# A new written-out order for the first stage of an attention and two-MLP kernel

## The chip, the cores and the metric

The kernel runs on one core of a Trainium2 chip. The time is the device time of one execution in microseconds (us). The engines are named as in the profile: PE multiplies matrices (PEld is its weight load, which runs beside it), DVE and ACT work on tiles elementwise, POOL is hardly used here, and SP issues the transfers (DMA). Each engine works through its own list of instructions in order and waits, where it must, for semaphores of the others.

## The reference

For 8 batches, 8 heads, 576 positions and 64 values a head, attention is computed inside chunks of 64 positions only. Its result, as 4608 rows of 512, goes through a gated MLP without an activation, and then through a second MLP with a leaky activation that has a slope per channel:

```
scores = q_c @ k_c.T / 8                 # per chunk of 64, F32
attn   = exp(scores - max); attn = attn / (sum + 1e-9)
x      = (attn @ v_c), heads side by side          # [4608, 512]
y      = (((x @ w1) * (x @ w2)) @ w3) @ w_out      # d_ff 1024
h      = y @ w_in                                  # d_ff 2048
out    = (max(h, 0) + alpha * min(h, 0)) @ w_out2
```

The weights arrive as 64-bit floats.

## The kernel before

Rows are handled in 9 blocks of 512. A **unit** is half a block of attention (256 rows); units 0 and 1 make block 0, units 2 and 3 block 1, and so on. Every product of two matrices is done in three passes over operands that are split in a high and a low half, so one 128-row group of a projection is 4 x 3 = 12 matmuls of 128x512. The operand pair of a block's attention is the tile `x`, of which there are two; block 2's `x` is block 0's buffer and can be written only when block 0's projections are done.

The work up to the first `acc` matmul, the **first stage**, follows a table of steps, `STARTUP`, that is written out by hand. Each step is a letter and an index:

- attention of unit u: `S` scores (PE), `M` maximum (DVE), `X` 16 exps (ACT), `Y` the division (DVE), `T` transpose (PE), `P` copy of the transposed (ACT), `V` product with v (PE), `c` high half of `x` (ACT), `d` low half of `x` (DVE). `q` issues a unit's loads. The order S M X Y T P V c d is a chain.
- weight granule i, a conversion from 64-bit floats: `A` (ACT, also issues the load of granule i+2), `B` (DVE, three instructions), `C` (ACT), `D` (DVE, two), `E` (DVE, two). There are 40: 0 to 15 are w1 and w2, 16 to 23 w_out, 24 to 39 w3. The raw bits of at most three granules are in memory at a time, so granule i+3 can be loaded when `D` of granule i is done.
- block b, group f: `a` and `b` (PE, 12 matmuls each, products with w1 and w2), `k` (ACT copies `a` out), `m` (DVE multiplies, SP writes the result to DRAM). `a` of group f needs granule 2f, `b` granule 2f+1. Blocks 0 to 2 are done here, 48 such groups of 12.
- `h` f.half (PE, 12 matmuls each, 16 in all) folds w3 and w_out into one matrix `wc`, with granule 24+2f+half; `s` and `w` (ACT, DVE) copy it out.

After the table, block 0's results are loaded again (`load_g`), and the `acc` matmuls begin. From there PE is kept in the order of the program; before that point the compiler's scheduler may move instructions on every engine, so that the table is a proposal. The queue of SP is one, in order, too. The first loads come unit by unit:

```
    for u in range(4):
        load_unit(u)
        if u < RAW:
            convert_load(u)
```

The v of a unit is loaded in six pieces, since for odd head pairs the two halves of the rows change places; exps and the product with v (`h2 ^ (a & 1)`, `h2 ^ odd`) follow that.

Of the kernel before, what the change touches and what calls it, by code (L numbers as in the profile page):

```python
# [34 lines left out]

STARTUP = """
    S0 M0 X0 A0 S1 Y0 M1 T0 P0 B0 X1 V0 D0 c0 Y1 C0 A1 d0 T1 A2 E0 P1 S2 B1 V1 A3 c1 M2 C1 d1 X2 D1 S3 B2 a0.0 M3 C2
    Y2 X3 E1 T2 D2 b0.0 B3 P2 Y3 k0.0 V2 C3 A4 m0.0 T3 c2 E2 P3 d2 a0.1 A5 D3 B4 V3 k0.1 E3 C4 c3 D4 b0.1 A6 d3 q4
    q5 E4 a1.0 m0.1 A7 B5 a0.2 k1.0 B6 C5 D5 C6 b1.0 D6 k0.2 E5 E6 A8 b0.2 m1.0 A9 B7 a1.1 m0.2 C7 D7 B8 a0.3 k1.1
    E7 C8 D8 A10 b1.1 k0.3 B9 E8 C9 b0.3 m1.1 A11 D9 B10 a1.2 m0.3 C10 E9 a0.4 k1.2 D10 A12 B11 b1.2 k0.4 E10 C11  # L40
    D11 A13 b0.4 m1.2 E11 B12 A14 a1.3 m0.4 C12 D12 a0.5 B13 k1.3 E12 C13 b1.3 D13 k0.5 A15 B14 E13 b0.5 C14 m1.3
    A16 D14 a1.4 m0.5 E14 B15 A17 a0.6 k1.4 B16 C15 D15 b1.4 C16 k0.6 D16 E15 b0.6 m1.4 A18 E16 B17 a1.5 A19 m0.6
    C17 D17 a0.7 k1.5 B18 E17 C18 b1.5 k0.7 D18 A20 B19 b0.7 m1.5 C19 E18 D19 A21 a1.6 m0.7 E19 S4 B20 k1.6 A22 b1.6
    M4 C20 D20 X4 B21 a1.7 m1.6 E20 b1.7 D21 k1.7 C21 Y4 A23 m1.7 T4 E21 P4 B22 A24 V4 B23 C22 c4 D22 C23 d4 E22 S5
    D23 A25 M5 E23 X5 B24 B25 D24 C24 C25 Y5 A26 E24 T5 P5 D25 h0.0 A27 B26 E25 C26 V5 D26 A28 h0.1 c5 B27 d5 C27 s0
    E26 a2.0 w0 A29 D27 h1.0 k2.0 B28 E27 C28 b2.0 D28 A30 B29 h1.1 m2.0 C29 E28 D29 A31 a2.1 s1 B30 w1 C30 E29 h2.0
    k2.1 D30 A32 B31 b2.1 E30 C31 D31 A33 h2.1 m2.1 E31 a2.2 s2 B32 A34 w2 C32 D32 h3.0 k2.2 B33 E32 C33 b2.2 D33
    A35 B34 h3.1 m2.2 C34 E33 D34 a2.3 A36 s3 B35 w3 C35 h4.0 E34 k2.3 D35 A37 b2.3 B36 E35 C36 h4.1 m2.3 A38 D36
    B37 a2.4 s4 E36 C37 w4 A39 h5.0 D37 k2.4 B38 E37 b2.4 C38 D38 B39 h5.1 m2.4 C39 E38 a2.5 s5 D39 w5 E39 h6.0 k2.5
    b2.5 h6.1 m2.5 a2.6 s6 w6 h7.0 k2.6 b2.6 h7.1 m2.6 a2.7 s7 w7 b2.7 k2.7 m2.7  # L50
# [8 lines left out]
def tile_attention_moe_moe(ctx: ExitStack, tc: tile.TileContext, qkv: bass.AP, w12: bass.AP,  # L59
# [150 lines left out]

    x_t = {}
    un = {}

    def load_unit(u):
# [4 lines left out]
        else:  # L219
# [3 lines left out]
                 "e": granule(slots[3], "e", F32).rearrange("p j (a h k) -> p j a h k", a=4, h=2)}  # L223
        v = un[u]["v"]
        for j in range(2):
            nc.sync.dma_start(out=un[u]["qk"][j], in_=qkv[2 * u + j, :, 0:2])
        for j in range(2):
            vs = qkv[2 * u + j, :, 2].rearrange("p (a x) -> p a x", a=4)
            nc.sync.dma_start(out=v[:, j, 0::2], in_=vs[:, 0::2])
            nc.sync.dma_start(out=v[0:D, j, 1::2], in_=vs[D:P, 1::2])  # L230
            nc.sync.dma_start(out=v[D:P, j, 1::2], in_=vs[0:D, 1::2])

    def attn_scores(u, where="att"):
        s = un[u]["s"] = pair(where, "sc")
        for j in range(2):
            q, k = (un[u]["qk"][j][:, i].rearrange("p (a c s) -> p a c s", a=4, c=2) for i in range(2))
            for a in range(4):
                for h2 in range(2):
                    for c in range(2):
                        r0, c0, to = D * h2, D * c, (4 * j + a) * D  # L240
                        matmul(s[c0:c0 + D, h2, to:to + D], q[r0:r0 + D, a, c], k[r0:r0 + D, a, c],
                                         start=True, stop=True)

    def attn_max(u):
        mx = un[u]["mx"] = work.tile([P, 2, 8], F32, tag="mx", name="mx")
        nc.vector.tensor_reduce(out=mx, in_=un[u]["s"].rearrange("p h (a k) -> p h a k", k=D), axis=AX.X, op=ALU.max)
        nc.vector.tensor_scalar_mul(mx, mx, -SCALE)  # L247

    def attn_exp(u, tiles=range(2)):
# [4 lines left out]
        for j in tiles:  # L254
            for a in range(4):
                for h2 in range(2):
                    n, h = 4 * j + a, h2 ^ (a & 1)
                    nc.scalar.activation(out=e[:, j, a, h], in_=s[:, h2, n * D:(n + 1) * D], func=AF.Exp,  # L258
                                         bias=mx[:, h2, n:n + 1], scale=SCALE, accum_out=sm[:, j, a, h:h + 1])

    def attn_softmax(u):
        e, sm = un[u]["e"].rearrange("p j a h k -> p (j a h) k"), un[u].pop("sm").rearrange("p j a h -> p (j a h)")
        nc.vector.tensor_scalar_add(sm, sm, 1e-9)
        nc.vector.reciprocal(sm, sm)
        nc.vector.tensor_tensor(out=e, in0=e, in1=sm.unsqueeze(2).to_broadcast([P, 16, D]), op=ALU.mult)

    def attn_transpose(u, where="att"):
        e = un[u]["e"]
        pa = un[u]["pa"] = pair(where, "pa")
        for j in range(2):  # L270
            for a in range(4):
                transpose(pa[:, j, a * P:(a + 1) * P], e[:, j, a].rearrange("p h k -> p (h k)"), ident)

    def attn_copy(u):
        pt = un[u]["pt"] = work.tile([P, 2, 4, 2, D], F32, tag="pt", name="pt", bufs=1)
        nc.scalar.copy(pt.rearrange("p j a c s -> p j (a c s)"), un[u]["pa"])

# [12 lines left out]
    def attn_out(u, lo):  # L290
# [25 lines left out]
    def fold_split(f, lo):  # L316
        if not lo:
            wc_g[f] = granule(24 + f, "wc")
        dst, ps = wc_g[f], ab["fold"][:, f % 2]
        if lo:  # L320
            nc.vector.tensor_tensor(out=dst[:, LO], in0=ps, in1=dst[:, HI].bitcast(F32), op=ALU.subtract)
        else:
            nc.scalar.copy(dst[:, HI], ps)
# [6 lines left out]
    def product(b, f, a, ps):  # L330
        nc.vector.tensor_tensor(out=a, in0=ps, in1=a, op=ALU.mult)  # L331
# [38 lines left out]
    def proj2(b, f):  # L370
# [6 lines left out]
        nc.vector.tensor_scalar(out=g, in0=ps, scalar1=0.0, scalar2=alpha_sb[:, f:f + 1], op0=ALU.min, op1=ALU.mult)  # L377
        nc.vector.scalar_tensor_tensor(out=g, in0=ps, scalar=0.0, in1=g, op0=ALU.max, op1=ALU.add)  # L378
# [99 lines left out]
    for b in range(LEAD, NB):  # L478
        parts = [p for i in range(2) for p in unit_steps(2 * (b + 1) + i, False)] if b + 1 < NB else []
        for f in range(NF1):  # L480
# [5 lines left out]
            nc.scalar.copy(a, pa)  # L486
# [80 lines left out]
```

## Time and profile before

| what | us |
|---|---|
| median of 3 runs (1537.49 to 1541.13) | 1538.48 |
| the profiled execution | 1539.19 |
| span in it, first to last instruction | 1537.4 |
| PE busy in it | 1494.1 |
| DVE busy | 780.4 |
| ACT busy | 422.6 |

The times come from unprofiled executions, the rows below from one profiled execution, whose own time is 1.8 us over its span. PE is busy for 97% of the span; the rest, and the stretches in which PE ran at the lower of its two clocks, lie almost all in the first 320 us.

### The profile page before, as it was taken

What the parts mean: (1) busy time and instruction counts of PE and PEld (TensorE: products, weight loads), DVE (VectorE), ACT (ScalarE), POOL (GpSimd) and SP (SyncE); (2) the same over time, 40 slices, a digit from 0 to 9 for tenths busy, and PEclk for the clock granted to TensorE, in tenths of its full rate; (3) what the DMA queues carried; (4) which work ended last, traced back from release to release, by engine and by line L of the source; (5) the groups of instructions that cost most, each with busy time, mean ns of one, the idle gap of its engine ahead of it and who ended that gap; (6) DMA issues with size and microseconds to landing.
All of it is one profiled execution on the core that took longest, in us unless ns stands there. A gap on an engine that the chain in (4) does not pass through costs nothing.

```text
span 1537.4 us, 21112 instructions
## 1 busy us (share of the span) xinstructions
PE 1494.1 (97%) x8688; PEld 1231.1 (80%) x8688; DVE 780.4 (51%) x1250; ACT 422.6 (27%) x1107; POOL 0.7 (0%) x6
## 2 busy tenths in 40 slices
PE   4997999999999999999999999999999999999998
PEld 3785787788888888888888888888888888888887
DVE  4989963366667665331334344343434344343433
ACT  6535323444444443331211111111111111111111
POOL 0000000000000000000000000000000000000000
PEclk9998999999999999999999999999999999999999
DMA  8644425644545456236501000010101000000000
GB/s 249 190 165 151 136 98 165 192 153 155 188 163 192 151 179 206 83 103 199 165 0 55 1 20 36 1 55 0 56 0 38 18 7 35 1 28 0 28 1 28
DMA packets 65041, 141.89 MB, mean 92 GB/s; under 512 B 6833, under 2 KB 25265, under 8 KB 64945
## 3 DMA queue, kind: packets, MB, share of 16 engines
q1 hardware_dynamic: 64944, 140.54, 27.7%
q8 instruction: 68, 1.11, 0.3%
q14 instruction: 29, 0.23, 0.0%
HBM read 98.57 MB, written 41.94 MB: 91 GB/s over the span
## 4 chain that ended last, share of the span: by engine, by line
PE 89%; DVE 4%; DMA 3%; ACT 2%; SPq 1%; issue 1%; ACTq 0%; DVEq 0%
PE acc L93 38%; PE a L93 23%; PE b L93 22%; PE wc L93 2%; PE ab L93 2%; DMA v<-in_qkv 1%; ACT e L258 1%; PE sc L93 1%; PE pa L93 1%; DMA raw<-in_wo 1%; DMA raw<-in_w 1%; PE pa L98 1%; DVE p L175 1%; DMA g<-g_dram 1%; DVE m L164 0%
## 5 line engine op out<-in xcount | busy, mean ns | idle before, releaser
L93 PE MATMUL acc<-w,gs 128*128 128x512 f32 x1728 | 414.7, 389 | 0.0
L93 PEld LDWEIGHTS acc<-w,gs 128*128 128x128 f32 x1728 | 324.4, 188 | 67.2
L104 ACT CAST gs<-g 128x512 fp32r<-128x512 f32 x168 | 104.6, 622 | 660.7 <-DVE g L378 635.0
L93 PE MATMUL acc<-gs,wc 128*128 128x512 f32 x864 | 210.2, 395 | 3.8 <-DVE gs L105 3.8
L93 PE MATMUL a<-y,w 128*128 128x512 f32 x864 | 207.5, 389 | 0.0
L93 PE MATMUL b<-y,w 128*128 128x512 f32 x864 | 207.5, 389 | 0.0
L93 PEld LDWEIGHTS acc<-gs,wc 128*128 128x128 f32 x864 | 161.6, 189 | 40.4 <-DVE gs L105 5.5
L93 PEld LDWEIGHTS b<-y,w 128*128 128x128 f32 x864 | 162.2, 188 | 33.7
L93 PEld LDWEIGHTS a<-y,w 128*128 128x128 f32 x864 | 162.2, 188 | 33.7
L105 DVE TENSOR_TENSOR gs<-g,gs 128x512 fp32r<-128x512 f32 x168 | 116.2, 692 | 134.7 <-ACT gs L104 132.7
L93 PE MATMUL a<-x,wa 128*128 128x512 f32 x720 | 175.1, 393 | 2.4 <-DVE x L297 2.4
L93 PE MATMUL b<-x,wa 128*128 128x512 f32 x720 | 175.7, 393 | 0.0
L93 PEld LDWEIGHTS a<-x,wa 128*128 128x128 f32 x720 | 136.3, 190 | 31.3 <-DVE x L297 2.9
L93 PEld LDWEIGHTS b<-x,wa 128*128 128x128 f32 x720 | 133.5, 188 | 27.6
L377 DVE TENSOR_SCALAR g<-b,alpha_sb 128x512 f32<-128x512 f32 x72 | 54.0, 750 | 177.7 <-PE b L93 177.7
L377 DVE TENSOR_SCALAR g<-a,alpha_sb 128x512 f32<-128x512 f32 x72 | 54.0, 750 | 162.6 <-PE a L93 162.6
L258 ACT ACTIVATE e<-sc,mx 128x64 f32<-128x64 f32 x288 | 85.7, 348 | 31.4 <-DVE mx L247 31.4
L331 DVE TENSOR_TENSOR a<-b,a 128x512 f32<-128x512 f32 x60 | 41.3, 688 | 95.1 <-PE b L93 84.4
L258 ACT ACTIVATION_READ_ACCUMULATOR e<-sc,mx 128x1 f32 x288 | 69.7, 242 | 0.0
L93 PE MATMUL ab<-x,wa 128*128 128x512 f32 x288 | 69.3, 390 | 0.0
L486 ACT COPY a<-a 128x512 f32<-128x512 f32 x48 | 28.6, 596 | 131.2 <-PE a L93 112.5
L93 PEld LDWEIGHTS ab<-x,wa 128*128 128x128 f32 x288 | 53.9, 188 | 11.2
(56 smaller groups left out, 995.9 us busy)
## 6 DMA issues: line engine op xcount, KB each, us to landing
qk<-in_qkv SPq DMA_DIRECT2D x36, 512.0 KB, 4.9
raw<-in_w2nd SPq DMA_DIRECT2D x32, 512.0 KB, 4.0
w_dram<-wm SPq DMA_DIRECT2D x32, 512.0 KB, 3.3
w<-w_dram SPq DMA_DIRECT2D x32, 512.0 KB, 3.3
y_dram<-y SPq DMA_DIRECT2D x36, 256.0 KB, 2.9
yraw<-y_dram SPq DMA_DIRECT2D x18, 512.0 KB, 4.3
out<-o SPq DMA_DIRECT2D x36, 256.0 KB, 2.1
raw<-in_w SPq DMA_DIRECT2D x16, 512.0 KB, 4.2
```

Source lines behind the costliest of these rows:

```text
L93: ins = nc.tensor.matmul(*args, **kw)
L98: ins = nc.tensor.transpose(*args, **kw)
L104: nc.scalar.copy(dst[:, HI], src)
L105: nc.vector.tensor_tensor(out=dst[:, LO], in0=src, in1=dst[:, HI].bitcast(F32), op=ALU.subtract)
L175: nc.vector.scalar_tensor_tensor(out=p, in0=conv_raw[i][:, :, 0], scalar=2.0 ** -52, in1=p, op0=ALU.mult, op1=ALU.mult)
L258: nc.scalar.activation(out=e[:, j, a, h], in_=s[:, h2, n * D:(n + 1) * D], func=AF.Exp, bias=mx[:, h2, n:n + 1], scale=SCALE, accum_out=sm ...
L331: nc.vector.tensor_tensor(out=a, in0=ps, in1=a, op=ALU.mult)
L377: nc.vector.tensor_scalar(out=g, in0=ps, scalar1=0.0, scalar2=alpha_sb[:, f:f + 1], op0=ALU.min, op1=ALU.mult)
L486: nc.scalar.copy(a, pa)
```

## The change

The table is written in a new order, and now DVE and ACT are kept to the program's order inside the first stage as PE is (the class `InOrder`, switched off for DVE and ACT after the table). Units 4 and 5 (steps S4 to V5) stand among block 0's and block 1's products, and their `c` and `d` behind block 0's last product. For units 0 to 3 (`u < CROSS`) v is loaded plainly, one transfer per tile, and the heads keep their places. The first loads are regrouped: queries and keys of two units and the first raw weights ahead of v. A first activation of one element (`warm`) brings the table of exps in at once. The folds `h` alternate between two pairs of banks (`att`, `p23`) and stand mostly at the end; the first two reloads of block 0's results (`g0`, `g1`) come before the last `s` and `w`.

```
 STARTUP = """
-    S0 M0 X0 A0 S1 Y0 M1 T0 P0 B0 X1 V0 D0 c0 Y1 C0 A1 d0 T1 A2 E0 P1 S2 B1 V1 A3 c1 M2 C1 d1 X2 D1 S3 B2 a0.0 M3 C2
...
+    S0 A0 M0 B0 X0 S1 D0 M1 A1 Y0 X1 B1 T0 D1 C1 Y1 P0 C0 V0 E1 A2 E0 T1 c0 B2 P1 d0 C2 V1 D2 E2 S2 c1 A3 d1 A4 M2
+    a0.0 B4 X2 b0.0 D4 B3 D3 a0.1 C4 Y2 C3 A5 k0.0 S3 E4 k0.1 E3 T2 M3 b0.1 P2 m0.0 B5 X3 D5 V2 m0.1 a0.2 c2 Y3 A6
...
+    class InOrder:
...
+            def call(*args, **kw):
+                ins = op(*args, **kw)
+                if self.on:
+                    tc.keep_in_program_order(ins)
...
+    CROSS = 4
...
+            if u < CROSS:
+                nc.sync.dma_start(out=v[:, j].rearrange("p a x -> p (a x)"), in_=qkv[2 * u + j, :, 2])
+                continue
...
-                    n, h = 4 * j + a, h2 ^ (a & 1)
+                    n, h = 4 * j + a, h2 ^ (a & 1 if u >= CROSS else 0)
...
-            if f % 2 == 0:
-                ab["fold"] = pair("p23", "wc")
-        ps = ab["fold"][:, f % 2]
+            ab["fold", f] = pair(("att", "p23")[f % 2], "wc")[:, 0]
+        ps = ab["fold", f]
...
+    act.activation(out=work.tile([P, 1], F32, tag="warm", name="warm", bufs=1), in_=ident[:, 0:1], func=AF.Exp)
     for u in range(4):
-        load_unit(u)
-        if u < RAW:
-            convert_load(u)
+        unit_tiles(u)
+    for load, n in ((load_qk, 0), (convert_load, 0), (load_qk, 1), (load_v, 0), (convert_load, 1), (load_v, 1),
+                    (load_qk, 2), (convert_load, 2), (load_v, 2), (load_qk, 3), (load_v, 3)):
+        load(n)
...
-    lent = {0: "att", 1: "p23", 2: "att", 3: "p23"}
+    lent = {1: "p23", 3: "p23", 5: "p23"}
...
-    pinned[0] = True
+    act.on = dve.on = False
     load_unit(2 * LEAD)
-    steps = [(b, f) for b in range(LEAD) for f in range(NF1)]
-    load_g(*steps[0])
-    load_g(*steps[1])
```

What stands in the lists of the engines follows at three places. First SP's queue at the start of the program (`qk` are queries and keys, `raw` raw weights); before:

```order
L226 DMA qk<-in_qkv 128x1024 x2
L229 DMA v<-in_qkv 128x2x128
L230 DMA v<-in_qkv 64x2x128
L231 DMA v<-in_qkv 64x2x128
L229 DMA v<-in_qkv 128x2x128
L230 DMA v<-in_qkv 64x2x128
L231 DMA v<-in_qkv 64x2x128
L143 DMA raw<-in_w 128x1024
L226 DMA qk<-in_qkv 128x1024 x2
```

And of the change:

```order
L238 DMA qk<-in_qkv 128x1024 x2
L148 DMA raw<-in_w 128x1024
L238 DMA qk<-in_qkv 128x1024 x2
L244 DMA v<-in_qkv 128x512 x2
L148 DMA raw<-in_w 128x1024
L244 DMA v<-in_qkv 128x512 x2
L238 DMA qk<-in_qkv 128x1024 x2
```

Unit 1's queries and keys moved from ninth behind six pieces of v to the fourth transfer, and a unit's v is two transfers instead of six.

Next PE around units 4 and 5 (`sc` are scores, `pa` first the transpose, then the product with v, `a`, `b` and `ab` the products of blocks 0 to 2, `wc` the folds), before:

```order
L93 MATMUL b<-x,wa 128x512 x12
L93 MATMUL ab<-x,wa 128x512 x24
L98 MATMUL pa<-ident,e 128x128 x8
L93 MATMUL pa<-pt,v 64x64 x32
L93 MATMUL sc<-qk 64x64 x32
L93 MATMUL wc<-wo,w_1485 128x512 x12
L98 MATMUL pa<-ident,e 128x128 x8
L93 MATMUL wc<-wo,w_1571 128x512 x4
L93 MATMUL pa<-pt,v 64x64 x32
L93 MATMUL wc<-wo,w_1571 128x512 x8
L93 MATMUL a<-x,wa 128x512 x12
```

And of the change, where the scores of both units stand further ahead:

```order
L100 MATMUL a<-x,wa 128x512 x12
L100 MATMUL b<-x,wa 128x512 x12
L100 MATMUL pa<-ident,e 128x128 x16
L100 MATMUL ab<-x,wa 128x512 x12
L100 MATMUL pa<-pt,v 64x64 x32
L100 MATMUL ab<-x,wa 128x512 x12
L100 MATMUL pa<-pt,v 64x64 x32
L100 MATMUL a<-x,wa 128x512 x12
L100 MATMUL b<-x,wa 128x512 x12
L100 MATMUL ab<-x,wa 128x512 x24
```

The transposes and products with v of both units now have products of blocks 0 and 1 in front, between and behind; before, all products of blocks 0 and 1 were done by then.

Last PE at the end of the first stage (`acc` are the first matmuls after the table), of the change:

```order
L100 MATMUL b<-x,wa 128x512 x12
L100 MATMUL ab<-x,wa 128x512 x24
L100 MATMUL wc<-wo,w_2072 128x512 x12
L100 MATMUL wc<-wo,w_2095 128x512 x12
L100 MATMUL wc<-wo,w_2141 128x512 x12
L100 MATMUL wc<-wo,w_2205 128x512 x12
L100 MATMUL wc<-wo,w_2225 128x512 x12
L100 MATMUL acc<-gs,wc 128x512 x12
L100 MATMUL sc<-qk 64x64 x32
```

Before, a fold and a product took turns up to the end, and a product of block 2 stood directly ahead of `acc`; now five folds do.

## Rows read from the trace of the kernel before

**Rows 1.** Busy time of each engine by stretch, with PE's granted clock and DMA.
```profile
core 0: us, PE busy (x) PEld busy (x) DVE busy (x) ACT busy (x) POOL busy (x), PEclk, DMA share, GB/s
0.00:37.57 37.57, 15.71 (x400) 13.84 (x400) 17.93 (x32) 22.35 (x101) 0.70 (x6) 0.96 0.83 253
37.57:56.34 18.77, 17.59 (x199) 13.96 (x195) 16.48 (x31) 13.80 (x52) 0.00 (x0) 0.90 0.76 233
56.34:124.58 68.24, 68.24 (x300) 56.23 (x300) 62.73 (x122) 25.81 (x43) 0.00 (x0) 1.00 0.49 164
124.58:163.86 39.28, 27.33 (x343) 21.34 (x343) 37.53 (x72) 24.47 (x87) 0.00 (x0) 0.83 0.36 117
163.86:242.90 79.04, 79.04 (x349) 65.15 (x347) 50.65 (x94) 20.88 (x35) 0.00 (x0) 1.00 0.43 138
242.90:245.30 2.40, 0.01 (x2) 0.00 (x1) 1.44 (x3) 1.82 (x3) 0.00 (x0) 1.00 0.39 144
245.30:319.12 73.82, 72.65 (x548) 58.09 (x549) 26.66 (x39) 29.33 (x94) 0.00 (x0) 0.98 0.49 153
319.12:1537.40 1218.28, 1213.55 (x6557) 1002.50 (x6555) 567.02 (x862) 284.14 (x694) 0.00 (x0) 1.00 0.22 74
```

**Rows 2.** The chain that ended last: start us, length us, engine and tile.
```profile
59.37 2.72 PE ab L93 x12
81.50 4.98 DMA raw<-in_w
146.94 4.84 ACT e L258 x32
249.90 1.09 PE sc L93 x64
267.54 0.87 PE pa L98 x8
```

**Rows 3.** Timeline of PE, to 40 us: start, length, work [idle before <-releaser].
```profile
4.42 1.13 PE L93 MATMUL sc<-qk 64*64 64x64 f32 x32 [4.42 <-DMA qk<-in_qkv]
5.78 1.13 PE L93 MATMUL sc<-qk 64*64 64x64 f32 x32 [0.23 <-DMA qk<-in_qkv]
12.62 1.14 PE L93 MATMUL sc<-qk 64*64 64x64 f32 x32 [5.71 <-DMA qk<-in_qkv]
...
35.65 1.99 PE L93 MATMUL sc<-qk 64*64 64x64 f32 x64 [4.18 <-DVE x L297]
37.57 4.74 PE L93 MATMUL a<-x,wa 128*128 128x512 f32 x12
```

**Rows 4.** What DMA moved in 0 to 37 us, in 40 equal slices.
```profile
GB/s 0 31 217 350 412 344 227 142 248 261 332 399 395 338 231 247 266 215 412 412 351 235 246 267 279 332 394 379 328 193 95 226 213 310 390 407 133 0 0 18
```

**Rows 5.** Timeline of DVE and ACT, first instructions.
```profile
6.98 1.23 DVE L246 TENSOR_REDUCE mx<-sc 128x16 f32<-128x1024 f32 x1 [6.98 <-PE sc L93]
...
8.50 1.28 ACT L258 ACT_TABLE_LOAD   x1 [8.50 <-DVE mx L247]
```

**Rows 6.** Timeline of PE, 140 to 250 us.
```profile
142.54 1.98 PE L93 MATMUL sc<-qk 64*64 64x64 f32 x64 [3.21 <-DVE x L297]
...
149.97 4.39 PE L93 MATMUL wc<-wo,w 128*128 128x512 f32 x10 [3.02 <-DVE w L180]
...
245.30 4.60 PE L93 MATMUL acc<-gs,wc 128*128 128x512 f32 x12 [2.39 <-DVE gs L105]
```

**Rows 7.** Groups by line, 0 to 245 us: busy us, mean ns | idle before <-releasers.
```profile
L164 DVE SCALAR_TENSOR_TENSOR m<-raw,m 128x512 uint32<-128x512 uint32 x40 | 27.5, 687 | 0.6
L155 ACT ACTIVATE m<-raw 128x512 f32<-128x512 f32 x40 | 27.2, 697 | 33.0 <-DMA raw<-in_w3t 13.1 <-DMA raw<-in_wo 9.9 <-DMA raw<-in_w 9.7
L161 DVE TENSOR_SCALAR m<-m 128x512 f32<-128x512 f32 x40 | 16.6, 419 | 5.6 <-ACT m L155 5.6
...
L246 DVE TENSOR_REDUCE mx<-sc 128x16 f32<-128x1024 f32 x6 | 7.3, 1217 | 7.0 <-PE sc L93 7.0
...
L300 ACT CAST x<-pa 128x1024 fp32r<-128x1024 f32 x6 | 6.2, 1027 | 1.1 <-PE pa L93 0.9
```

More of the change, by code (lines that the diff above doesn't have):

```diff
@@ L42 @@
[L42 to L46, printed above, removed]
@@ new lines @@
+    k1.5 E16 b1.5 A18 B17 B18 C17 V4 D18 a1.6 C18 A19 m1.5 E18 b1.6 B19 k1.6 D17 C19 a0.6 E17 m1.6 D19 b0.6 k0.6 E19
+    A20 a0.7 m0.6 B20 A21 B21 C20 b0.7 k0.7 A22 D21 C21 E21 a1.7 c4 m0.7 c5 d4 b1.7 d5 k1.7 D20 E20 a2.0 m1.7 B22
+    b2.0 k2.0 D22 C22 E22 A23 a2.1 B23 A24 m2.0 C23 B24 b2.1 k2.1 D24 C24 A25 D23 a2.2 B25 E23 C25 b2.2 k2.2 m2.1
+    D25 E25 a2.3 m2.2 E24 A26 b2.3 B26 k2.3 D26 C26 h0.0 E26 m2.3 A27 B27 h0.1 A28 D27 C27 E27 A29 h1.0 s0 B29 w0
+    h1.1 D29 C29 E29 A30 B28 a2.4 s1 w1 C28 D28 b2.4 k2.4 E28 B30 h2.0 m2.4 C30 D30 E30 h2.1 A31 B31 A32 D31 C31
@@ L51 @@
+    h3.0 s2 B32 A33 D32 C32 a2.5 B33 D33 C33 b2.5 k2.5 E31 E32 h3.1 w2 m2.5 E33 h4.0 s3 A34 w3 B34 A35 h4.1 D34 C34
+    E34 A36 a2.6 B36 s4 D36 C36 w4 h5.0 k2.6 E36 A37 B35 b2.6 D35 C35 E35 a2.7 m2.6 B37 D37 C37 b2.7 k2.7 E37 A38
+    B38 h5.1 A39 m2.7 D38 h6.0 B39 s5 C38 w5 E38 h6.1 C39 D39 E39 h7.0 s6 w6 h7.1 g0 g1 s7 w7
 """
@@ L205, in mm3, with unit_tiles @@
         for i, (s, m) in enumerate(PASSES):
-            matmul(ps, stat(s), mov(m), start=first and i == 0, stop=last and i == 2)
+            pe.matmul(ps, stat(s), mov(m), start=first and i == 0, stop=last and i == 2)
+    CROSS = 4
     x_t = {}
     un = {}
-    def load_unit(u):
+    def unit_tiles(u):
         if u < 4:
@@ L223, in load_unit, with load_qk, load_v @@
                  "e": granule(slots[3], "e", F32).rearrange("p j (a h k) -> p j a h k", a=4, h=2)}
+    def load_unit(u):
+        unit_tiles(u)
+        load_qk(u)
+        load_v(u)
+    def load_qk(u):
+        for j in range(2):
+            nc.sync.dma_start(out=un[u]["qk"][j], in_=qkv[2 * u + j, :, 0:2])
+    def load_v(u):
         v = un[u]["v"]
         for j in range(2):
-            nc.sync.dma_start(out=un[u]["qk"][j], in_=qkv[2 * u + j, :, 0:2])
-        for j in range(2):
+            if u < CROSS:
+                nc.sync.dma_start(out=v[:, j].rearrange("p a x -> p (a x)"), in_=qkv[2 * u + j, :, 2])
+                continue
             vs = qkv[2 * u + j, :, 2].rearrange("p (a x) -> p a x", a=4)
@@ L318, in fold_split @@
             wc_g[f] = granule(24 + f, "wc")
[L319 removed]
+        dst, ps = wc_g[f], ab["fold", f]
         if lo:
[L321 removed]
+            dve.tensor_tensor(out=dst[:, LO], in0=ps, in1=dst[:, HI].bitcast(F32), op=ALU.subtract)
         else:
[L323 removed]
+            act.copy(dst[:, HI], ps)
     def proj1(b, f, which, ps):
@@ L420, in tile_attention_moe_moe @@
             a = ab[tuple(rest)][2] = tmp("a")
-            nc.scalar.copy(a, ab[tuple(rest)][0])
+            act.copy(a, ab[tuple(rest)][0])
         elif kind == "b":
@@ L430, in tile_attention_moe_moe @@
             fold_split(n, kind == "w")
+        elif kind == "g":
+            load_g(*steps[n])
     def unit_steps(u, cut):
```

87 lines of the change are left out of this document (41 added, 46 removed).

## The prediction

> **What bounds the kernel now.** I read the stretches first [rows 1]. From 319 us to the end PE is busy for 1213.6 of 1218.3 us at the full clock, and the change moves nothing there; the reader is to see that only the first 320 us can give or take anything. PE's work there is the same before and after, so I count how long it should take. One group of 12 matmuls takes 2.72 us at the full clock, a unit's scores 1.09, its transposes 0.87 [rows 2], its product with v as long as the scores. The first stage has 48 products and 16 folds, 64 x 2.72 = 174.1, and six units, 6 x 3.05 = 18.3: 192.4 us. It ends at 242.9. So 50.5 us are lost, and the stretches say where:
>
> - to 37.57: only seven eighths of four units' attention (8.3 us) done: 29.3 lost, PE idle or at the lower clock (the first group after it takes 4.74 instead of 2.72 [rows 3]);
> - 37.57 to 56.34: 15.1 of work in 18.8, 3.7 lost;
> - 56.34 to 124.58 and 163.86 to 242.9: PE without a hole, about 0.3 lost;
> - 124.58 to 163.86: 22.4 of work (six groups and both last units) in 39.3, 16.9 lost. Every product of blocks 0 and 1 is done by then, so PE waits for the chain of units 4 and 5 and then for granules: 3.21 for DVE's low half of x, 3.02 for a granule [rows 6], and the clock falls (0.83).
>
> Behind it 2.4 us pass until the reloaded result is split, and the first acc group then takes 4.60 instead of 2.72, 1.9 more [rows 6].
>
> DVE is nearly as loaded: 186.8 us busy to 245.3 (the first six stretches [rows 1]) against PE's 192.4.
>
> **The change, part by part.**
>
> *The front, to a0.0.* Before, the first unit's scores start at 4.42 and 5.78, but the second's first half only at 12.62, after 5.71 us of waiting for its queries [rows 3]: six pieces of v and a raw granule lie ahead of it in SP's queue. Two wide tiles of 512 KB landed 1.36 us apart, 385 GB/s, and the slices show 400 when wide tiles move and 215 to 270 between [rows 4]. With the new queue the order is two tiles of queries, raw 0, two tiles, v (plain, two tiles), raw 1: at 385 GB/s from 3.06 on (4.42 less 1.36), unit 1's queries are in at 9.9, raw 1 at 12.6. Now the chain, handovers about 0.1: M0 7.0 to 8.4 [rows 5]; X0 can start at 8.5 instead of 9.8, since the table of exps is loaded already, and takes 4.8 with its 16 exps [rows 2] (32 records), to 13.2; A1 0.7 (L155 [rows 7]) to 13.9; X1 to 18.7; Y1 (1.2 and two short ones, 1.7) to 20.4. C1, then P0 (1.03, as L300) to 20.2; V0 2.0 at the lower clock (as the 1.99 of unit 3's scores [rows 3]) to 22.3; T1 to 24.2; P1 to 25.3; V1 to 27.4; c1 1.03 to 28.5; d1 1.2 to 29.8. DVE has 20.5 us of work up to there and is not what holds. a0.0 starts at **29.9 instead of 37.57**; done by then are 7.2 us of work (three units' scores, two transposes, two products with v), so 22.7 are lost.
>
> The bounds: if the plain tiles moved at the front's mean rate of 253 GB/s [rows 1], raw 1 would land at 17.6 and everything behind 4.4 later, a0.0 at 34.3. I take 385, because the tiles ahead of S1 and X1 are wide.
>
> *The table of exps.* The row has 1.28 us for the load, and the exp follows at once, so that 1.3 us leave the path [rows 5]. The Trainium skill (ScalarE: Activation LUTs, What ACT_TABLE_LOAD costs) counts a drain of 1.38 with each load, 2.66 in all; by that the sum below would be 1.4 lower. No drain is seen before the first exp here, and I stay with the row.
>
> *a0.0 to b0.4.* The first group again at the lower clock: 2.0 lost. Then I followed the two lists. T2 waits for nothing: Y2 is done at 38, PE arrives at 41.0. S3 ends at 41.0, M3 42.5, X3 (behind P2) 43.0 to 47.7, Y3 to 49.4; PE reaches T3 at 48.4: 1.1 lost. S4 needs the banks that unit 2 leaves with d2 (50.6): 0.3. V3 waits for P3, which stands behind A6, A7, C5 and k0.2: 0.6. b0.2 needs granule 5, E5 at 54.6 behind d2, B6 and D6: 1.2. Together 3.2. From there PE's and DVE's lists run within 1 to 2 us of each other: b0.4 ends at 73.9.
>
> *Units 4 and 5.* Their chains now have products of blocks 0 and 1 beside them. S5 stands eight groups ahead of T5 (21.8 us; M, X, Y need 1.4 + 4.8 + 1.7 = 7.9), and between b0.7, which frees block 0's x, and a2.0 stand two groups, 5.4 us: c4 and c5 take 2 x 1.03, d4 and d5 end about 1.3 behind c5, 3.7 in all. So the 16.9 lost there go, as long as DVE reaches m0.7 in time. It then costs nothing; without that cover each us that DVE is late costs one.
>
> *DVE's budget.* No DVE instruction is added. Of its work 20.5 us lie ahead of a0.0, and 1.4 (the last two w) behind the last granule. From both sides: 186.8 busy as before leaves 165 us, and E39 at 195; all durations end to end, 40 granules x (4 x 0.687 + 3 x 0.419 [rows 7]) = 160.2, 32 products and folds x 0.69, 18 of 1.22 and 18 short ones, make 208, and E39 at 216. PE reaches h7.1, which needs E39, at about 217. The new table puts a granule's steps back to back, each reading what the last wrote, so I take 214, near the upper end: 3 us of slack, and 1.2 more lost to small waits that I cannot place.
>
> *Raw loads.* Three raw granules: load i+3 can go when D of granule i is done. One lands in 4.98 [rows 2], A takes 0.7, 5.7 together; in the new order at least two granules' DVE work, 8 us, usually lie between, for granule 20 only 5.2 (D17, then E17, m1.6, D19, E19, m0.6, B20). That costs under 1 us, once.
>
> *The end of the stage.* 22.7 + 2.0 + 3.2 + 1.2 = 29.1 lost, so h7.1 ends at 192.4 + 29.1 = 221.5, say **222 instead of 242.9**, 20.9 less. g0 and g1 are issued behind D38 and the last raw loads, some 10 us ahead of need, so the 2.4 of waiting and the 1.9 at the lower clock fall away. New: acc writes the banks of fold 7, which s7 and w7 (0.6 + 0.7 and handovers) free 1.5 after h7.1, while PE gets there after half a group, 1.36: 0.3 with the rest. Unit 6's queries now load only when h7.0 has read its granules, and its six pieces of v stand ahead of g2: queries land about 5.4 after h7.0, needed at 5.7; g2 is split at about 10, needed at 9.6. I take 0.8 for both; at worst, with a landing as late as 4.98 behind a full queue, 3. Sum: 4.3 - 1.1 = 3.2 less.
>
> *The plain v.* The same number of exps, matmuls and multiplications; only the place of a head changes. Nothing on the engines.
>
> *Sum.* 20.9 + 3.2 = 24.1 less than the profiled execution's 1539.2: 1515.1. That execution was 0.7 over the median, so I say **1515** for the median, with 1510 to 1520 as the likeliest case's own range.
>
> **The rivals.**
>
> *DVE idles as it does now.* Between 56.34 and 163.86 DVE was busy 100.3 of 107.5 us, idle 6.8% [rows 1]. At that rate it idles 12.7 us in the 187 from a0.0 to h7.1; less the 3 of slack and the 1.2 counted, h7.1 ends 8.5 later: 1524. For it: the list is now fixed and in order, so that a late A or C holds everything behind. Against: of the idle time up to 245 only 5.6 is a wait for A (L161 [rows 7]). The same price covers the x of block 2 coming late.
>
> *Slower: the raw loads set the pace.* ACT waited 33.0 us for raw granules [rows 7], and with ACT held in order the exps, P and k stand behind such a wait. It decides the sign when a load needs more than about 8.0 us to land, 0.7 more than lies between, 0.7 lost per granule: 40 x 0.7 = 28 eats the 24.1 and the slack. At 1 us per granule: 1515 - 3 + 40 = 1552. Against it: 4.98 is the row.
>
> *No change:* the front is held by its chain of exps and not by the loads, and units 4 and 5 wait at another place; it would need both 7.6 and 16.9 to come back: 1538.
>
> *Better:* the 3.2 and 1.2 do not occur (DVE's durations overlap as before) and the loads land sooner: 1508.
>
> **How the numbers follow.** The forecast 0.70, DVE idle 0.17, better 0.06, no change 0.03, raw loads 0.04. The range 1508 to 1525 takes in the first three. A measurement of this kernel can tell about 0.2%, 3 us: faster 0.93, same 0.03, slower 0.04.
>
> **What the changed profile would show.** a0.0 at 29 to 31; S1 near 8.5 and no table load beside X0; holes of PE of 1 to 2 us before T3 and b0.2; no hole over 2 us and no fall of the clock between 75 and 220; DVE's busy total higher by up to 20 us; the first acc group near 222 in 2.9. Wrong would be: a0.0 later than 34 (the rate), DVE idle over 8 us between 75 and 220 (the first rival), ACT waiting longer than now for raw granules (the second), or PE idle around 225 for g2.

## The result: slower, and the profile after

The changed kernel takes **1557.85 us** (median of 4 runs, 1557.59 to 1558.4) against 1538.85 of the kernel before beside it (4 runs, 1537.49 to 1541.13): a ratio of **1.0122, 95% interval 1.0105 to 1.014**. Forecast was 1515 with a range of 1508 to 1525. The time is outside the range, on the other side of no change.

The stretches of the profiled execution after (its time 1558.09 us, span 1556.3), cut at the places that answer to [rows 1]: first product `a0.0`, the stretch around `b1.5`, first `acc`, block 3's first `a`. Behind the two times stand the length of the stretch, the busy time of each engine with its instructions, PE's granted clock, the DMA engines' busy share and GB/s:

```profile
0.00:30.89 30.89, 14.74 (x337) 13.13 (x337) 20.17 (x34) 19.44 (x78) 0.70 (x6) 1.00 0.84 310
30.89:103.62 72.73, 72.14 (x600) 57.73 (x601) 67.70 (x119) 42.19 (x166) 0.00 (x0) 1.00 0.53 166
103.62:117.75 14.13, 11.39 (x169) 8.99 (x168) 11.49 (x22) 7.17 (x11) 0.00 (x0) 0.88 0.29 95
117.75:229.91 112.16, 112.16 (x488) 90.08 (x481) 99.63 (x177) 37.80 (x64) 0.00 (x0) 1.00 0.45 150
229.91:304.38 74.47, 72.60 (x549) 56.65 (x548) 26.77 (x39) 30.03 (x95) 0.00 (x0) 1.00 0.54 168
304.38:1556.30 1251.92, 1247.28 (x6557) 1001.64 (x6555) 567.24 (x862) 284.34 (x694) 0.00 (x0) 1.00 0.21 72
```

Against [rows 1] the first `acc` stands 15.4 us earlier (229.91 for 245.30), the stretch behind it takes 0.65 more (74.47 for 73.82), and the rest, which the forecast held for untouched, takes **33.6 more** (1251.92 for 1218.28). The sum is the 18.9 by which the span grew. In that last stretch PE has hardly a hole (1247.28 busy of 1251.92) and a granted clock of 1.00, as before: it is busy longer with the same matmuls. The chain that ended last (start, length, what) shows with which; first in the first stage, then late in the kernel:

```profile
63.29 2.80 PE a L100 x12
...
85.69 1.09 PE sc L100 x64
...
1299.86 2.80 PE a L100 x12
1302.66 2.80 PE acc L100 x12
1305.46 2.80 PE b L100 x12
```

The kernel before, late as well:

```profile
1301.76 2.72 PE acc L93 x12
1304.48 2.72 PE b L93 x12
```

A group of 12 matmuls of 128x512 takes **2.80 us where it took 2.72** (there, and in [rows 2]); 64 scores take 1.09 as before. The reader is to see that the busy share hides this: PE is 98% busy on the page, 97% before, and idles less than before (26.0 us for 43.3, span less busy time). There are 6240 such matmuls, 520 groups: 520 x 0.08 = 41.6 us (with the two digits of a row, 36 to 47).

### The profile page after: what moved, and what is told of

The parts are those of the page before. It is cut to its first block, busy times and chain, and to the rows that moved or that the text cites. A ratio compares the mean times of both kernels' runs of the same rounds, so it can differ in the third digit from the quotient of the medians.

```text
span 1556.3 us, 21102 instructions
## 1 busy us (share of the span) xinstructions
PE 1530.3 (98%) x8688; PEld 1228.2 (79%) x8688; DVE 793.0 (51%) x1250; ACT 421.0 (27%) x1108; POOL 0.7 (0%) x6
## 4 chain that ended last, share of the span: by engine, by line
PE 95%; DVE 2%; ACT 2%; DMA 1%; issue 0%; SPq 0%; ACTq 0%
PE acc L100 38%; PE b L100 24%; PE a L100 23%; PE ab L100 4%; PE wc L100 3%; PE pa L100 2%; PE sc L100 1%; ACT e L100 1%; DMA g<-g_dram 1%; DVE m L100 0%; DMA qk<-in_qkv 0%; DVE mx L100 0%; DVE p L100 0%; DVE e L100 0%; DVE x L100 0%
## 5 line engine op out<-in xcount | busy, mean ns | idle before, releaser
L100 PE MATMUL acc<-w,gs 128*128 128x512 f32 x1728 | 426.5, 396 | 0.0
L100 PE MATMUL acc<-gs,wc 128*128 128x512 f32 x864 | 213.8, 398 | 2.1 <-DVE gs L100 2.1
L100 PE MATMUL b<-y,w 128*128 128x512 f32 x864 | 213.0, 395 | 0.0
L100 PE MATMUL a<-y,w 128*128 128x512 f32 x864 | 213.0, 395 | 0.0
L100 PE MATMUL b<-x,wa 128*128 128x512 f32 x720 | 180.0, 398 | 0.1
L100 DVE TENSOR_SCALAR m<-m 128x512 f32<-128x512 f32 (+1 forms) x144 | 60.9, 424 | 67.1 <-ACT m L100 65.7
L100 ACT COPY a<-a 128x512 f32<-128x512 f32 x60 | 35.9, 599 | 151.2 <-PE a L100 132.5
```

Of the source, the lines that this page charges most:

```text
L100: ins = op(*args, **kw)
```

## The experiments: what made a matmul slower

The one new piece of memory in the change is the tile `warm`, one element per partition, which takes a slot of 32 bytes. It is the first tile of the pool `work`, so that all of `work` (`x`, `y`, `gs`, the reloaded weights) moves by 32 bytes. In every matmul of 128x512 one operand lies in `work` and the other in the pool of the granules. (Both operands of the scores lie among the granules, at a distance that no run changed, so that their 1.09 says nothing here; the products with v read one operand from each pool.) The table gives for each kernel where the program as built puts the first granule and `x` (bytes in a partition), their distance modulo 2048 and what that leaves over a multiple of 256, the time of a group in the trace (from the start of one to the start of the next), and the median of the runs (one execution where the number of runs is 1). The bytes themselves stand in no trace, but the distance can be added up from the kernel: 131072 bytes of granules and 33024 of other tiles of `work` ahead of `x` make 164096, 256 over a multiple of 2048, and each added tile moves that by its slot:

| kernel | granule | x | distance | rest to 256 | group, us | median, us (runs) |
|---|---|---|---|---|---|---|
| before | 17088 | 181184 | 256 | 0 | 2.72 | 1538.85 (4) |
| after | 17088 | 181216 | 288 | 32 | 2.80 | 1557.85 (4) |
| e1 | 17088 | 181248 | 320 | 64 | 2.75 to 2.80 | 1541.48 (10) |
| e2 | 17088 | 181216 | 288 | 32 | 2.80 | 1576.11 (4) |
| e3 | 17152 | 181376 | 384 | 128 | 2.79 to 2.80 | 1554.61 (4) |
| e4 | 17120 | 181248 | 288 | 32 | 2.80 | 1557.75 (1) |
| e5 | 17088 | 181184 | 256 | 0 | 2.72 | 1518.6 (4) |
| e6 | 17088 | 181440 | 512 | 0 | 2.72 | 1517.44 (1) |
| e7 | 17120 | 181216 | 256 | 0 | 2.72 | 1520.92 (1) |
| e8 | 17088 | 181952 | 1024 | 0 | 2.72 | 1516.94 (1) |
| d1 | 17216 | 181312 | 256 | 0 | 2.72 | 1517.44 (1) |
| d2 | 17088 | 181376 | 448 | 192 | 2.76 to 2.80 | 1554.06 (1) |
| d3 | 17088 | 181568 | 640 | 128 | 2.79 to 2.80 | 1552.91 (1) |

The kernel before, beside them, took 1538.15 us (median of 13) with e1 to e4, 1538.57 (7) with e5 to e8, 1539.57 (one run) with d1 to d3 and 1539.25 (7) with n1 to n4.

**e2: is it the place, or anything else in the change?** The kernel before, with an unused slot of 32 bytes:

```
+    nc.gpsimd.memset(work.tile([P, 8], F32, tag="pad", name="pad", bufs=1), 0.0)
     for u in range(4):
```

> The kernel before, with an unused tile of 32 bytes per partition put first into the pool work (POOL clears it once), so that every other tile of work begins 32 bytes later; order, loads and pinning as before. Theory A: groups take 2.80 from the start; 520 x 0.08 = 41.6, less what the holes of the first stage hide, 1572 to 1580. Rival B: groups of 2.72, 1539.

Measured: 1576.11, ratio 1.0251 (1.0232 to 1.0269). The timeline of PE (start, length, line, operation, operands, count), late in this kernel, has starts 2.80 apart:

```profile
1300.83 2.96 PE L93 MATMUL b<-y,w 128*128 128x512 f32 x12
1303.63 2.96 PE L93 MATMUL acc<-w,gs 128*128 128x512 f32 x12
1306.43 2.96 PE L93 MATMUL a<-y,w 128*128 128x512 f32 x12
```

The slot alone costs the kernel before 38.0 us; order, pinning and loads have no part in it.

**e1 and e3: must `work` start at a multiple of 64 bytes, or of 128?** The tile `warm` is made larger, in e3 with a second pad ahead of the granules:

```
-    act.activation(out=work.tile([P, 1], F32, tag="warm", name="warm", bufs=1), in_=ident[:, 0:1], func=AF.Exp)
@@ e1 @@
+    act.activation(out=work.tile([P, 16], F32, tag="warm", name="warm", bufs=1), in_=ident[:, 0:16], func=AF.Exp)
@@ e3 @@
+    act.activation(out=work.tile([P, 32], F32, tag="warm", name="warm", bufs=1), in_=ident[:, 0:32], func=AF.Exp)
+    nc.gpsimd.memset(const.tile([P, 16], F32, name="pad"), 0.0)
```

> The changed kernel with the one-element tile warm made 64 bytes long per partition, so that every tile of the pool work begins 64 bytes later than in the kernel before instead of 32; nothing else differs. Theory A (place in memory: the 32-byte shift of the pool work makes every 128x512 matmul slower): a group of 12 takes 2.72 us again instead of 2.80, from the first stage to the end; 520 groups x 0.08 = 41.6 less, so about 1557.9 - 41 = 1517, first acc group near 225. Rival B (something in the new order or in the pinning of ACT and DVE makes the matmuls slower): groups stay at 2.80, 1558.

> As e1_warm64, with 64 bytes more in front of the large granules and 64 more in front of work, so that both begin at a multiple of 128 bytes (in the kernel before both begin 64 past one). Theory A with a step of 64 bytes: as e1_warm64, 1517. Theory A with a coarser step: groups below 2.72, down to 512 columns at 2.4 GHz, 12 x 0.2133 = 2.56, so 1517 - 520 x 0.16 = 1434 at the least. Rival B: 1558.

Measured: e1 1541.48, ratio 1.0023 (1.0013 to 1.0033); e3 1554.61, 1.0107 (1.0092 to 1.0123). Neither gives 2.72 back. e1 is a mixture, seen in two pieces of PE's timeline: the groups of the first start 2.75 apart, those of the second 2.80:

```profile
640.76 2.91 PE L100 MATMUL b<-x,wa 128*128 128x512 f32 x12
643.51 2.91 PE L100 MATMUL acc<-gs,wc 128*128 128x512 f32 x12
646.25 2.91 PE L100 MATMUL a<-x,wa 128*128 128x512 f32 x12
...
1300.37 2.96 PE L100 MATMUL acc<-w,gs 128*128 128x512 f32 x12
1303.17 2.96 PE L100 MATMUL b<-y,w 128*128 128x512 f32 x12
```

e1 fits none of its theories; e3 lies near rival B's 1558, but e2 rules that rival out. A start of `work` at a multiple of 64 or of 128 is thus not enough.

**e4: move the granules too.** `warm` of 32 bytes as `[P, 8]`, and a pad of 32 bytes ahead of the granules, so that both operands move and the distance stays at 288:

```
+    nc.gpsimd.memset(const.tile([P, 8], F32, name="pad"), 0.0)
```

> As e1_warm64, but the granules begin 32 bytes later and work at the same multiple of 64 as in e1_warm64: the other operand is shifted. Each group reads one operand from the granules and one from work. Theory A, either operand counts: 2.80 everywhere, 1558. Theory A, only work counts: 2.72, 1517. Theory A, only the moving operand counts: 2.80 where the moving one lies in the granules (folds and the last product, acc<-w,gs, 160 groups), 2.72 elsewhere, about 1530. Rival B: 2.80, 1558.

Measured: 1557.75 (one run), groups still 2.80. So the place of `x` alone does not decide: e1 has it at the same byte and is the mixture. Two theories were left, one of the granules' own place and one of the distance between the operands. The next four tell them apart.

**e5 to e8: the distance.** e5 writes `warm` into a buffer that exists anyway, so that everything lies as before; e7 is e5 with the pad of e4, so that granules and `x` both lie 32 bytes from a place that was fast, at the old distance; e6 and e8 widen `warm` to 256 and 768 bytes:

```
@@ e5, e7 @@
+    act.activation(out=work.tile([P, 2, 8], F32, tag="mx", name="warm")[:, 0, 0:1], in_=ident[:, 0:1], func=AF.Exp)
@@ e7 @@
+    nc.gpsimd.memset(const.tile([P, 8], F32, name="pad"), 0.0)
@@ e6 @@
+    act.activation(out=work.tile([P, 64], F32, tag="warm", name="warm", bufs=1), in_=ident[:, 0:64], func=AF.Exp)
@@ e8 @@
+    act.activation(out=work.tile([P, 192], F32, tag="warm", name="warm", bufs=1)[:, 0:128], in_=ident[:, 0:128], func=AF.Exp)
```

> The changed kernel with the first activation writing into a buffer of the tag mx, which exists anyway, so that x, y, gs, the folded weights and the granules lie at exactly the addresses of the kernel before. In e1_warm64 a 64-byte shift gave groups of 2.75 and 2.80, in e3_all128 and e4_gran32 2.79 and 2.80. Theory A' (the distance between the operand in work and the one in the granules sets the cadence, and the kernel before has a good one, 256 bytes past a multiple of 2048): 2.72 everywhere, about 1517 (the sum of the prediction, 1515, would then stand). Theory A'' (the changed order also slows matmuls): 2.75 to 2.80, 1541 to 1558.

> The changed kernel with warm made 256 bytes long: the distance of work's operands to the granules is 512 past a multiple of 2048 (before: 256, changed: 288). Theory A' with a period of 256 bytes: 2.72, 1517. If the addresses of work alone count and not the distance: unknown, 2.75 to 2.80 as in e1_warm64.

> As e5_same_places, but granules and work both begin 32 bytes later, so that the distance is 256 as before and every address is off by 32. Theory A' (distance): 2.72, 1517. If the addresses themselves count (multiples of 64): 2.80, 1558.

> As e6_apart512 with 768 bytes in front of work: the distance is 1024 past a multiple of 2048. Theory A' with a period of 256: 2.72, 1517; with a period of 2048 and a best place near 256: 2.75 to 2.80.

Measured: e5 1518.6, ratio **0.9871 (0.9855 to 0.9888)**; e6 1517.44, e7 1520.92, e8 1516.94 (one run each). All four have 2.72. e7 has `x` at 181216 as the changed kernel has it, and the granules at 17120 as e4 has them, and is fast; its timeline of PE:

```profile
1302.35 2.88 PE L101 MATMUL a<-y,w 128*128 128x512 f32 x12
1305.07 2.88 PE L101 MATMUL acc<-w,gs 128*128 128x512 f32 x12
1307.79 2.88 PE L101 MATMUL b<-y,w 128*128 128x512 f32 x12
```

Neither place counts by itself; the distance does.

**d1 to d3: is a multiple of 256 the rule?** d1 is e5 with a pad of 128 bytes ahead of the granules (`[P, 32]`), d2 and d3 have `warm` at 192 and 384 bytes (`[P, 48]`, `[P, 96]`).

> As e5_same_places, with granules and work both 128 bytes later: every address is off by half of 256, the distance stays 256. If the distance alone sets the cadence: 2.72, 1517 to 1521. If an address counts by its rest to 256 (e6 and e8 kept work's rest of 192): 2.75 to 2.80, 1540 to 1558.

> The changed kernel with warm made 192 bytes long: the distance is 448, three quarters of the way between the two good ones (256 and 512), and x lies at the same address as in e3_all128. Period of 256: slower than 2.72, by the mirror image of 320 (e1_warm64) 2.75 to 2.80, 1541 to 1558. Period of 64 with another cause in e1_warm64: 2.72, 1517.

> The changed kernel with warm made 384 bytes long: the distance is 640, which is 512 and half of 256 more. Period of 256: as e3_all128 (384), 2.79 to 2.80, 1555. Period of 128 (and e3_all128 slow for its own addresses): 2.72, 1517.

Measured (one run each): d1 1517.44 with 2.72, d2 1554.06, d3 1552.91 with up to 2.80. Distances 256, 512 and 1024 are fast; 288, 320, 384, 448 and 640 are not. A larger distance by itself is no help (640), and moving both operands by 128 costs nothing (d1). One restriction: the stationary operand steps by 512 bytes from tile to tile, so that each group runs through all four distances that agree modulo 512. The distances 512 and 1024 are then the same case, and what is shown fast are two: a rest to 512 of 0 and one of 256. Each row with one run rests on its trace, in which every such group shows the cadence, more than on its time.

## The experiments: what the new order itself is worth

**e5** answers this as well, since only places tell it from the changed kernel. Its stretches (columns as above):

```profile
0.00:31.28 31.28, 15.06 (x337) 13.28 (x337) 20.31 (x34) 19.43 (x78) 0.70 (x6) 1.00 0.85 313
31.28:102.88 71.60, 70.96 (x600) 57.71 (x601) 66.95 (x118) 42.21 (x166) 0.00 (x0) 1.00 0.52 166
102.88:116.78 13.90, 11.16 (x170) 9.10 (x168) 12.05 (x23) 7.08 (x11) 0.00 (x0) 0.88 0.30 96
116.78:226.51 109.73, 109.56 (x487) 89.96 (x481) 99.72 (x177) 37.90 (x64) 0.00 (x0) 1.00 0.45 152
226.51:298.86 72.35, 71.19 (x549) 56.76 (x548) 26.50 (x39) 29.80 (x95) 0.00 (x0) 1.00 0.56 175
298.86:1517.20 1218.34, 1213.56 (x6557) 1002.17 (x6555) 566.99 (x862) 284.09 (x694) 0.00 (x0) 1.00 0.22 74
```

The last stretch is 1218.34 again, as in [rows 1]; the first `acc` stands 18.8 us earlier than before, the next stretch gives 1.5. Behind the front, the one stretch with PE idle and a lower granted clock (0.88) is 102.88 to 116.78. In PE's timeline there a group waits for ACT (the brackets give the idle time ahead and what ended it), and takes 4.41 instead of 2.98 us:

```profile
104.54 2.98 PE L100 MATMUL ab<-x,wa 128*128 128x512 f32 x12
107.45 1.16 PE L100 MATMUL pa<-pt,v 64*64 64x64 f32 x64
111.35 4.41 PE L100 MATMUL ab<-x,wa 128*128 128x512 f32 x12 [2.74 <-ACT a L100]
115.69 1.16 PE L100 MATMUL pa<-pt,v 64*64 64x64 f32 x64
```

And ACT's timeline at the same place:

```profile
108.74 1.01 ACT L100 COPY pt<-pa 128x1024 f32<-128x1024 f32 x1 [2.92 <-PE pa L100]
109.64 0.66 ACT L100 ACTIVATE m<-raw 128x512 f32<-128x512 f32 x1
110.20 0.61 ACT L100 CAST wo<-m 128x512 fp32r<-128x512 f32 x1
110.71 0.59 ACT L100 COPY a<-ab 128x512 f32<-128x512 f32 x1
```

The group is `b1.5`; the copy that it waits for is `k1.5`, which only reads `a1.5`. The two groups fill two halves of one tile, so the reading is that the write of `b1.5` waits until the other half has been read; n3 tests it. `k1.5` stands in ACT's list behind P4, A17 and C16, and P4 waits 2.92 us itself, so that it comes late.

**n3: `k1.5` behind `b1.5`**, with the places of e8:

```
-    k1.5 E16 b1.5 A18 B17 B18
+    E16 b1.5 k1.5 A18 B17 B18
```

> As e8_apart1024, with one step of the table moved: k1.5 (ACT copies a1.5 out) behind b1.5 instead of ahead of it, as it stands at most other groups that use the pair p01. In e5_same_places b1.5 waits 2.74 us for ACT there and its group then runs at 4.4 instead of 2.9. Theory (the compiler makes b wait for k, since both halves are one tile): the hole of 2.74 and the slow group go, 3 to 4.5 less than e8_apart1024: 1513 to 1514. Rival (something else that ACT does then is waited for): same hole, 1517.

Measured: **1514.87** (4 runs, 1514.33 to 1515.12), ratio **0.9844 (0.9827 to 0.986)**, the fastest here; 3.7 less than e5, and 2.1 less than e8 (one run), where 3 to 4.5 had been expected. The traces separate the two parts: from `a0.0` to the first `acc` there are 195.23 us in e5, 193.83 in e8, where the hole of 2.73 was there but the group behind it took 3.01, and 191.13 in n3. The hole is worth 2.7, the slow group 1.4 where it came. PE's timeline of n3 has neither:

```profile
106.81 1.16 PE L100 MATMUL pa<-pt,v 64*64 64x64 f32 x64
107.90 3.02 PE L100 MATMUL ab<-x,wa 128*128 128x512 f32 x12
110.85 1.16 PE L100 MATMUL pa<-pt,v 64*64 64x64 f32 x64
```

**n1: without the line `warm`.** It is removed and nothing put in its place.

> The changed kernel without the first activation and its tile; nothing else differs, and work's operands fall back to the distance of 256 from the granules. Distance theory: groups of 2.72, and the table of exps is loaded beside the first exp again, so 1.3 us (the 1.28 of the row) over e5_same_places: about 1520, 38 less than the changed kernel for one line less. If a drain went with the load, 2.7 over: 1521. Order theory (already weak after e5_same_places): 1558.

Measured: 1519.18, ratio 0.9868 (0.9854 to 0.9883), as e5. ACT's timeline of n1 shows the load of the table at 0.73 all the same, far ahead of the first exp, which starts at 8.42:

```profile
0.73 1.28 ACT L100 ACT_TABLE_LOAD   x1 [0.73 <-PEq L577]
7.82 0.66 ACT L100 ACTIVATE m<-raw 128x512 f32<-128x512 f32 x1 [5.80 <-DMA raw<-in_w]
8.42 0.32 ACT L100 ACTIVATE e<-sc,mx 128x64 f32<-128x64 f32 x1
```

The 1.3 us over e5 that were expected for a load beside the first exp have no cause here, then; the 0.6 measured are within the scatter of either's runs. So `warm` bought nothing that these runs show, and cost 39 us. A0 stands first on ACT in the new order, and the load goes with it; before it stood at 8.50, in front of the exps [rows 5].

**n2: the old first loads** on e5, with v in six pieces:

```
-    CROSS = 4
+    CROSS = 0
...
+        load_unit(u)
+        if u < RAW:
+            convert_load(u)
```

> As e5_same_places, with the first loads unit by unit again and v in six pieces for units 0 to 3 (the old order of loads and of heads). The prediction's front: S1 near 12.6 instead of 9.1, a0.0 some 5 to 7 us later than the 31.3 of e5_same_places, and the stretch behind cannot give it back, since PE is without holes from there: 1523 to 1526. Rival (the front is held by the chain of exps): within 2 us of e5_same_places, 1519.

Measured: 1522.82, ratio 0.9896 (0.9882 to 0.9911). Unit 1's scores wait 4.61 us for their queries again, and `a0.0` starts at 34.20 instead of 31.28, 2.9 later where 5 to 7 were expected:

```profile
11.59 1.13 PE L100 MATMUL sc<-qk 64*64 64x64 f32 x32 [4.61 <-DMA qk<-in_qkv]
...
24.79 1.98 PE L100 MATMUL pa<-pt,v 64*64 64x64 f32 x64 [5.22 <-ACT pt L100]
...
34.20 3.02 PE L100 MATMUL a<-x,wa 128*128 128x512 f32 x12 [0.96 <-DVE x L100]
...
49.40 1.16 PE L100 MATMUL pa<-pt,v 64*64 64x64 f32 x64
```

The regrouped loads and the plain v are together worth 4.2 us (1522.82 less 1518.6; 3.6 against n1, which ran beside it), 2.9 of them ahead of `a0.0`. The rest of the 6.3 by which `a0.0` moved (37.57 [rows 3] to 31.28) came with the rest of the change and is not taken apart, except that it is not the pinning: n4 below has `a0.0` at 31.16.

The rows also show that the plain v has a price. With the heads in their places the 64 matmuls of a product with v take about twice as long. In e5:

```profile
20.09 3.68 PE L100 MATMUL pa<-pt,v 64*64 64x64 f32 x64 [2.90 <-ACT pt L100]
...
44.87 2.08 PE L100 MATMUL pa<-pt,v 64*64 64x64 f32 x64
```

V2 fills 2.01 us there (44.87 to the next start, 46.88) and 1.09 in n2 (49.40 to 50.49), both at a granted clock of 1.00; V3 likewise, and V0 fills 3.61 for 1.91. Units 4 and 5, whose heads cross in every kernel, take 1.09. By the kernel's loops the crossed form takes the four pairings of a half of the rows with a half of the columns in turn, the plain form only two of them; that this is the reason was not tested. No run has the regrouped loads with crossed heads.

**n4: ACT and DVE not kept in order** (e5 with `act.on = dve.on = False` from the start).

> As e5_same_places, with ACT and DVE left to the scheduler in the first stage as in the kernel before (PE stays in the program's order). If pinning these two engines is a part of the gain: PE has more holes in the first stage, 1521 to 1530. If the new table and the loads give all of it: 1517 to 1520. If pinning costs (a late A or C holds what stands behind it): below 1516.

Measured: 1516.27, ratio 0.9853 (0.9838 to 0.9867), 2.3 less than e5 (the intervals of the two ratios overlap), between two of the expected bands. Left to the scheduler, the hole at `b1.5` is 0.60 instead of 2.74, and from `a0.0` to the first `acc` there are 192.10 us for e5's 195.23:

```profile
110.20 3.04 PE L100 MATMUL ab<-x,wa 128*128 128x512 f32 x12 [0.60 <-ACT a L100]
```

No gain by pinning is seen; it turned one badly placed step of the table into a wait. With that step moved, the pinned n3 needs 191.13 us for the same stretch.

## Why the prediction was wrong, point by point

- **The step that failed** is the first: "From 319 us to the end PE is busy for 1213.6 of 1218.3 us at the full clock, and the change moves nothing there", and with it the 2.72 us of a group, carried over to the changed kernel in every sum. The change moved no instruction there, but it moved the operands: 2.80. The size and the cause are shown (e2 with the place alone, e5 without it): of the 42.9 us between 1515 and 1557.85, 39.3 are the places (1557.85 less e5's 1518.6). No rival had the mechanism; the line `warm` was counted for the load that it brings forward and at nothing for its tile. That the rival *raw loads* named 1552, near the measured time, is chance: ACT waited 5.7 us for raw granules in the changed kernel, 33.0 before [rows 7].
- **With the places restored** the sum holds: e5 1518.6 for 1515, and n3, with one step moved, 1514.87, both inside 1508 to 1525. That it comes so close is in part luck, since misses cancel: V0 and the wait at `b1.5` cost more than worked out, the first group and the holes less (below). By the profiled executions, e5 saves 20.3 of the 24.1 (1539.19 less 1518.94), n3 24.9 (less 1514.33).
- **The front** came as worked out up to V0: in e5 S1 at 9.12 ("near 8.5"), T0 at 15.25 (15.0 by its 13.2 and 1.7), V0 at 20.09 (20.2). Then V0 took 3.61 for the 2.0 of the sum, and `a0.0` stood at 31.28 (29.9, bounds 29.9 and 34.3). "Nothing on the engines" was thus wrong of the plain v, and the 1.4 by which `a0.0` was late is less than V0's 1.6. The slow clock forecast for the first group, 2.0 us, did not come, which pays for it: starts 2.87 apart at once, not 4.74 [rows 3]. (The 8.3 us of work done by 37.57 before are right, as four units' scores, two transposes and two products with v; "seven eighths" is not, they are two thirds of 12.2.) In e5's timeline of PE:

```profile
31.28 3.03 PE L100 MATMUL a<-x,wa 128*128 128x512 f32 x12 [1.44 <-DVE x L100]
34.15 2.88 PE L100 MATMUL b<-x,wa 128*128 128x512 f32 x12
...
50.40 1.07 PE L100 MATMUL pa<-ident,e 128*128 128x128 f32 x8 [0.51 <-DVE e L100]
...
54.63 3.40 PE L100 MATMUL b<-x,wa 128*128 128x512 f32 x12
```

- **The holes**: before T3 0.51 (forecast 1.1), before `b0.2` none (forecast 1.2). That `b0.2` starts at 54.63, for 54.6 by E5, is chance: it starts where V3 ends (52.62 and 2.01). The longer V2 and V3 fill time in which n2, with V2 and V3 at 1.09, has PE waiting, 1.48 us before T3 and 1.03 in `b0.2`.
- **The table of exps**: the 1.28 left the path, with `warm` and without it (n1). Whether a drain goes with the load beyond its row, no run tells, since the load was back on the path in none.
- **Units 4 and 5**, "It then costs nothing", was wrong by 4.1 us: 2.74 of waiting and 1.39 at the lower clock (4.41 less 3.02). I had followed their chain and DVE, not ACT's list, where their P stands ahead of a copy that PE waits for. (S5 also stands six groups ahead of T5 and not eight; their 16 us still cover the 7.9.) n3 takes the loss away: first `acc` at 221.73 where "near 222" was forecast.
- **DVE idles** (the first rival): its price did not come, though its sign did. DVE was idle for 12.6 of the 145 us between 75 and 220 of e5, over the 8 that were to tell, but PE hardly waited for it. The waits of PE between 31.28 and 226.51 of e5 (what waited for whom, us in total, times, longest) are few; 2.1 us are DVE's, 1.4 of them ahead of `a0.0` itself:

```profile
PE ab L100 <- ACT a L100: 2.7, 1, 2.7
PE a L100 <- DVE x L100: 1.4, 1, 1.4
PE pa L100 <- DVE e L100: 0.5, 1, 0.5
PE wc L100 <- DVE w L100: 0.2, 1, 0.2
```

  DVE's busy total rose to 792.5 in e5 (793.0 in the changed kernel) from 780.4, inside the 20 forecast.
- **Raw loads, no change**: not seen; ACT waits 5.9 us for raw granules in e5, 5.6 of them for the first, against 33.0 [rows 7], and from 116.78 to 226.51 PE is busy for 109.56 of 109.73 us.
- **Behind the first stage**: in e5 the first `acc` group starts with no wait for g0 and at a granted clock of 1.00, as worked out, and fills 3.15 us (226.51 to 229.66) instead of 4.5; the 2.4 ahead of it are gone and the stretch behind gives 1.5, 3.9 together for the 3.2 of the sum.

What stays open is the memory's part in it: which access is delayed at the distances that are not a multiple of 256 bytes, why a rest of 64 costs a third as much for some pairs of operands (2.75), and whether more than the first tiles of the two pools counts, as the mixtures of e1 and d2 suggest. Open too is what the regrouped loads would give without the plain v's slower products.

## What to carry to other kernels

Cost a new tile by what it moves as well as by what it does: where PE is the bound, compare the time of one group of matmuls before and after, first of all, since neither busy shares nor waits show a matmul that has become slower. In this kernel a scratch tile was harmless in a buffer that exists (e5) or in a slot of a multiple of 256 bytes (e6, e8); behind the operands it should be too, which was not run. Where an order is fixed by hand on several engines, look at each copy out of a tile that another group still has to write, in the list of its own engine. And when a layout is simplified for the loads, compare the time of the matmuls that read it.

## What the runs showed of the hardware

- At a granted clock of 1.00 a group of 12 matmuls of 128x512 takes 2.72 us when stationary and moving operand lie a multiple of 256 bytes apart (distances 256, 512 and 1024, six kernels of the table), and 2.75 to 2.80 at the distances 288, 320, 384, 448 and 640. The products with v, 64 matmuls of 64x64 with one operand from each pool, fill 1.09 in e5 (254.00 to 255.09) and in the changed kernel (291.98 to 293.07) alike.
- The same 64 matmuls fill 2.01 us instead of 1.09 when the heads keep their places (V2 of e5 and of n2, granted clock 1.00).
- The load of the table of exps went with ACT's first activation at 0.73 us although that activation itself waited for its operand until 7.82 (n1).
- In the changed kernel's first loads 18 slices in a row, from 7 to 24 us, show 383 to 434 GB/s, near the 385 that was taken from [rows 3]; the line of what the DMA engines moved, in equal slices from 0 to 37 us:

```profile
GB/s 0 22 155 412 390 385 235 323 425 407 394 434 403 405 383 412 416 403 383 403 407 405 399 384 400 399 372 102 13 18 89 275 226 239 323 375 336 94 75 219
```
